# Second-stage matmuls of a fused attention and feed-forward kernel: 512 columns at once, or two times 256

## The chip, the core and the metric

The kernel runs on one core of one Trainium2 chip. The metric is the device time of one launch in microseconds (us). Five engines work side by side: TensorE (PE, matmuls; its weights loads are shown apart as PEld), VectorE (DVE), ScalarE (ACT), GpSimd (POOL) and SyncE (SP), which here only issues transfers. Data for the engines lie in on-chip memory; a matmul writes into accumulator banks, from which ScalarE and VectorE read the results.

## The reference

The reference computes a windowed attention over 8 batches, 8 heads, 576 positions and head size 64, in which a position sees itself and the 63 before it, and feeds the 4608 x 512 result through a feed-forward layer with a squared rectifier:

```python
scores = scale * np.matmul(q, k.transpose(0, 1, 3, 2))
mask = (rel >= 0) & (rel < window)              # window = 64
scores = np.where(mask, scores, -1000000000.0)
attn = np.exp(scores - np.max(scores, axis=-1, keepdims=True))
attn = attn / (np.sum(attn, axis=-1, keepdims=True) + 1e-09)
x = (attn @ v)  ->  4608 x 512
h = x @ w_in                                     # 512 x 2048
g = np.maximum(h, 0.0) ** 2
out = g @ w_out                                  # 2048 x 512
```

## The kernel before

The 4608 tokens are cut into 12 tiles of 384. A tile's feed-forward layer is 16 steps, one for each block of 128 hidden units. To keep accuracy with a fast one-pass number format (float32r), every factor is split into a high and a low part, and a product is the sum of three matmuls: high x high, high x low, low x high.

One step has two stages. In the **first stage** (`mm1`, line 352) twelve matmuls of 384 columns, four blocks of the 512 inputs with three products each, fill one bank, `h_ps`; the weights are blocks of `w_in`, and the tile's tokens stream past them. ScalarE takes the bank out with the rectifier (`r`, line 361), VectorE or ScalarE squares it (lines 366 and 364), ScalarE casts the high part (`ghi`, line 369) and VectorE subtracts to get the low part (`glo`, line 371). In the **second stage** (`mm2`, line 396) the blocks of 128 tokens of `ghi` and `glo` are the loaded weights, and the 512 columns of `w_out` stream past them: three token blocks with three products each, nine matmuls of 512 columns, each with a weights load of its own. They add up over the sixteen steps in three accumulators of 512 columns, one bank each: `oT` for the first token block and two buffers named `oV` for the others. After a tile's last step ScalarE copies each accumulator to `osb` (`put`, line 408), and SP sends it out (line 410). The streamed operand is read with its halves interleaved (`in_turn`), and the copies put the columns back in order (`by_half`, `ordered`).

TensorE also does the attention: scores (line 208), transposes of the probabilities (line 250) and products with the values (line 272). There are three such sections for each tile, and a section is worked into five steps of the feed-forward of an earlier tile.

Order: the first two tiles run in an order written out by hand (the string of tokens in the code), in which line 500 issues small filler matmuls on TensorE while data still arrive. From the third tile on, which is where the change acts, loops set the order. The second stage runs two steps behind the first: TensorE does `mm1` of step n, then the attention pieces of this step, then `mm2` of step n-2. Every engine works its instructions in the order in which they were issued; the weights load of a matmul is the one thing seen running beside the matmul ahead of it.

Of the kernel before, what the change touches and what calls it, by code (L numbers as in the profile page):

```python
# [24 lines left out]
def window_attention_relu2_ffn(ctx: ExitStack, tc: tile.TileContext, q, k, v, w_in, w_out, out):  # L25
    nc = tc.nc
    pe, dve, act, pool, sp = nc.tensor, nc.vector, nc.scalar, nc.gpsimd, nc.sync
    B, H, S, D = q.shape
    NT, DM = out.shape
# [3 lines left out]
    NF = DF // P  # L33
# [41 lines left out]
    wraw, wa, wparts = {}, {}, {}  # L75
# [299 lines left out]
    def in_turn(x):  # L375
        return x.rearrange("p (a b) -> p b a", a=2)

    def ordered(ps):
        return ps.rearrange("p (b a) -> p a b", a=2)

    def by_half(x):
        return x.rearrange("p (a b) -> p a b", a=2)

    hs, rg, gs, accs = {}, {}, {}, {}


    def mm2(t, f, ghi, glo):
        if f == 0 and t == 1:
            accs[t] = [ps_a.tile([P, 2, SW * P], F32, name=x)[:, n] for x, n in (("s_ps", slice(0, 2)), ("v_ps", 0))]
            accs[t] = [accs[t][0][:, 0], accs[t][0][:, 1], accs[t][1]]  # L390
        elif f == 0:
            accs[t] = [ps_o.tile([P, DM], F32, name="oV" if tb else "oT", bufs=2 if tb else 1) for tb in range(NTB)]
        for tb in range(NTB):
            ts = slice(tb * P, (tb + 1) * P)
            for n, (gg, part) in enumerate(((ghi, 0), (ghi, 1), (glo, 0))):
                pe.matmul(accs[t][tb], lhsT=gg[:, ts], rhs=in_turn(wparts[f][:, 1, part, :]),  # L396
                          start=f == 0 and n == 0, stop=f == NF - 1 and n == 2)
            if f == NF - 1 and t != 1:
                for op in "ZW":
                    put(op, t, tb)  # L400


    outs = {}

    def put(op, t, tb):
        if op == "Z":
            outs[t, tb] = wst.tile([P, DM], F32, name="osb", bufs=3)
            act.copy(by_half(outs[t, tb]), ordered(accs[t][tb]))
        else:
            sp.dma_start(out[t * TT + tb * P:t * TT + (tb + 1) * P, :], outs.pop((t, tb)))  # L410

# [93 lines left out]
    with tc.manual_schedule(engines={E.PE, E.DVE, E.Activation, E.Pool, E.SP}):  # L505
        for token in order.split():
            op, eng = token[0], token[-1] if token[-1] in "dap" else None
            n = int(token[1:].rstrip("dap"))
            if op in "LN":
                load_first("LN".index(op), n)  # L510
            elif op == "v":
                load_v(*divmod(n, (NB + 1) // 2))
            elif op == "w":
                fetch_w(n)
            elif op == "q":
                load_qk(1 + n // NPAIR, n % NPAIR)
            elif op == "D":
                turn(1 + n // NPAIR, n % NPAIR)
            elif op in "TU":
                ps_f[op, n] = turn_first("TU".index(op), *divmod(n, 2))  # L520
            elif op in "tu":
                copy_first("tu".index(op), *divmod(n, 2), ps_f[op.upper(), n], copier(eng))
            elif op == "K":
                idle(n)
            elif op in "abcdhl":
                weight(op, n)
            elif op == "M":
                hs[n] = mm1(*steps[n])
            elif op in "rpgG":
                evac(op, n, eng)  # L530
            elif op == "O":
                mm2(*steps[n], *gs.pop(n))
            elif op in "ZW":
                for tb in range(NTB):
                    put(op, steps[n][0], tb)
            else:
                section(op, n, eng)
# [4 lines left out]
    with tc.manual_schedule(engines={E.PE, E.DVE, E.Activation, E.Pool, E.SP}):  # L542
        for t in range(2, NTILE):
            for f in range(NF):
                n = NF * t + f
                m = min(f // 5, SPT - 1)
                hs[n] = mm1(t, f)
                evac("r", n)
                step(n, SPT * (t + 1) + m + 1, f - 5 * m)
                pend.append((n, t, f))  # L550
                done = pend.pop(0)
                mm2(*done[1:], *gs.pop(done[0]))
                if f != 5 * m:
                    for op in "pgG":
                        evac(op, n)
        for p in pend:
            mm2(*p[1:], *gs.pop(p[0]))
# [31 lines left out]
```

## Time and profile before

| what | value |
|---|---|
| median of 3 runs | 879.16 us (879.13 to 880.41) |
| span of the profiled execution | 878.4 us |
| TensorE matmuls: busy, count | 860.0 us, 6946 |
| TensorE weights loads: busy, count | 794.7 us, 6946 |
| VectorE, ScalarE, GpSimd busy | 452.0, 401.8, 50.1 us |
| mean granted TensorE clock | 0.996 |
| second-stage matmul of 512 columns, mean duration | 379 ns |
| first-stage matmul of 384 columns, mean duration | 327 ns |
| a 128x128 weights load, mean duration | 189 ns |

The profiled execution's own time is its span; the runs' median is 0.8 us above it. A matmul's duration in the profile reaches beyond the start of the next matmul, because they are pipelined; the distance from one start to the next is what adds up to time. In the groups, the columns are: line, engine, operation, output and inputs, shapes and count, then busy us and mean ns of one, then the idle time ahead of them and what ended it. In the timeline and the chain, the first number is the start in us from the beginning of the span and the second the length in us; several instructions in a row are merged, with their count.

### The profile page before, as it was taken

What the parts mean: (1) busy time and instruction counts of PE and PEld (TensorE: products, weight loads), DVE (VectorE), ACT (ScalarE), POOL (GpSimd) and SP (SyncE); (2) the same over time, 40 slices, a digit from 0 to 9 for tenths busy, and PEclk for the clock granted to TensorE, in tenths of its full rate; (3) what the DMA queues carried; (4) which work ended last, traced back from release to release, by engine and by line L of the source; (5) the groups of instructions that cost most, each with busy time, mean ns of one, the idle gap of its engine ahead of it and who ended that gap; (6) DMA issues with size and microseconds to landing.
All of it is one profiled execution on the core that took longest, in us unless ns stands there. A gap on an engine that the chain in (4) does not pass through costs nothing.

```text
span 878.4 us, 16976 instructions
## 1 busy us (share of the span) xinstructions
PE 860.0 (98%) x6946; PEld 794.7 (90%) x6946; DVE 452.0 (51%) x740; ACT 401.8 (46%) x1147; POOL 50.1 (6%) x70
## 2 busy tenths in 40 slices
PE   6799999999999999999999999999999999999998
PEld 5688998899999999999999999999999999999997
DVE  5799995754455444544455444453445544432222
ACT  5787875644344434434334444334434443432322
POOL 1210000210000000000000000000000000000000
PEclk9899999999999999999999999999999999999999
DMA  9989206460125002421033202141013200100100
GB/s 213 222 270 327 37 4 106 81 155 7 26 55 121 1 1 64 71 48 54 1 55 92 54 2 63 29 81 55 11 21 67 59 1 1 37 1 1 37 1 36
DMA packets 200302, 56.41 MB, mean 64 GB/s; under 512 B 185377, under 2 KB 193569, under 8 KB 200225
## 3 DMA queue, kind: packets, MB, share of 16 engines
q1 hardware_dynamic: 200224, 55.34, 27.4%
q8 instruction: 54, 0.88, 0.4%
q14 instruction: 24, 0.19, 0.1%
HBM read 45.88 MB, written 9.44 MB: 63 GB/s over the span
## 4 chain that ended last, share of the span: by engine, by line
PE 94%; SPq 3%; DMA 1%; ACT 1%; POOL 0%; DVE 0%; issue 0%; POOLq 0%
PE h_ps L352 42%; PE oV L396 26%; PE oT L396 14%; PE s_ps L208 3%; PE v_ps L272 3%; PE s_ps L396 2%; PE v_ps L250 1%; SPq L158 1%; PE v_ps L396 1%; SPq L130 1%; DMA w<-in_k_dram 1%; PE h_ps L500 0%; ACT sel L236 0%; SPq L80 0%; ACT r L361 0%
## 5 line engine op out<-in xcount | busy, mean ns | idle before, releaser
L352 PE MATMUL h_ps<-xhi,w 128*128 128x384 f32 x1536 | 407.0, 327 | 1.9 <-ACT r L361 1.4
L352 PEld LDWEIGHTS h_ps<-xhi,w 128*128 128x128 f32 x1536 | 275.2, 189 | 8.6 <-ACT r L361 3.3
L352 PE MATMUL h_ps<-xlo,w 128*128 128x384 f32 x768 | 250.6, 326 | 0.0
L361 ACT ACTIVATE r<-h_ps 128x384 f32<-128x384 f32 x192 | 93.6, 487 | 286.4 <-PE h_ps L352 285.7
L396 PE MATMUL oV<-w,ghi 128*128 128x512 f32 x704 | 209.5, 379 | 0.0
L366 DVE TENSOR_TENSOR r<-r 128x384 f32<-128x384 f32 x166 | 92.0, 554 | 165.4 <-ACT r L361 165.4
L371 DVE TENSOR_TENSOR glo<-r,ghi 128x384 fp32r<-128x384 f32 x192 | 107.8, 562 | 121.0 <-PE oV L396 82.0
L369 ACT CAST ghi<-r 128x384 fp32r<-128x384 f32 x192 | 98.8, 514 | 117.4 <-DVE r L366 115.4
L396 PEld LDWEIGHTS oV<-w,ghi 128*128 128x128 f32 x704 | 133.2, 189 | 18.8
L352 PEld LDWEIGHTS h_ps<-xlo,w 128*128 128x128 f32 x768 | 145.3, 189 | 4.8
L396 PE MATMUL oV<-w,glo 128*128 128x512 f32 x352 | 133.5, 379 | 0.0
L396 PE MATMUL oT<-w,ghi 128*128 128x512 f32 x352 | 110.2, 395 | 0.0
L236 ACT ACTIVATE sel<-sel,nm 128x64 f32<-128x64 f32 x272 | 90.8, 335 | 17.4 <-DVE nm L230 15.3
L396 PEld LDWEIGHTS oV<-w,glo 128*128 128x128 f32 x352 | 66.6, 189 | 9.4
L245 POOL TENSOR_TENSOR sel<-sel,rs 128x512 f32<-128x512 f32 x33 | 38.4, 1163 | 564.4 <-DVE rs L242 564.4
L396 PE MATMUL oT<-w,glo 128*128 128x512 f32 x176 | 66.8, 379 | 0.0
L254 DVE TENSOR_TENSOR pt<-v_ps,masks 128x1024 f32<-128x1024 f32 x31 | 38.0, 1224 | 46.8 <-PE v_ps L250 46.8
L396 PEld LDWEIGHTS oT<-w,ghi 128*128 128x128 f32 x352 | 59.0, 189 | 2.3 <-issue 0.2
L236 ACT ACTIVATION_READ_ACCUMULATOR sel<-sel,nm 128x1 f32 x272 | 50.9, 187 | 0.0
L140 DVE STREAM_TRANSPOSE qk<-raw 128x1152 f32<-128x1152 f32 x28 | 38.4, 1371 | 1.4 <-issue 1.4
L208 PE MATMUL s_ps<-qk 64*64 64x128 f32 (+1 forms) x1104 | 38.3, 276 | 0.1
L396 PEld LDWEIGHTS oT<-w,glo 128*128 128x128 f32 x176 | 33.3, 189 | 4.7
(80 smaller groups left out, 592.6 us busy)
## 6 DMA issues: line engine op xcount, KB each, us to landing
vt<-in_v_dram SPq DMA_DIRECT2D x144, 64.0 KB, 2.5
out_dram<-osb SPq DMA_DIRECT2D x36, 256.0 KB, 2.3
w<-in_moe_w_in_dram SPq DMA_DIRECT2D x16, 512.0 KB, 6.6
w<-in_moe_w_out_dram SPq DMA_DIRECT2D x16, 512.0 KB, 7.6
raw<-in_q_dram SPq DMA_DIRECT2D x112, 72.0 KB, 2.5
raw<-in_k_dram SPq DMA_DIRECT2D x112, 72.0 KB, 2.5
w<-in_q_dram SPq DMA_DIRECT2D x5, 256.0 KB, 4.6
w<-in_k_dram SPq DMA_DIRECT2D x5, 256.0 KB, 5.2
```

What stands on the lines that cost most here:

```text
L140: dve.transpose(get_turned(b, g // 2)[:, g % 2].rearrange("p n t -> p (n t)"), raw.rearrange("p n t -> p (n t)"))
L208: pe.matmul(ps[half * QB:(half + 1) * QB, j, w * P + c0:(w + 1) * P], lhsT=qk[r, 0, qb * QB:(qb + 1) * QB], rhs=qk[r, 1, k0:k0 + P - c0], ...
L236: act.activation(sels[i][:, w, hd], sels[i][:, w, hd], AF.Exp, bias=nms[i][:, n], scale=SCALE, accum_out=sums[i][:, n])
L245: (dve if eng == "d" else pool).tensor_tensor(p, p, rs[i][:, :, None].broadcast_to([P, SW * 2, QB]), ALU.mult)
L254: dve.tensor_tensor(pts[i].rearrange("p (w n) q -> p w n q", n=2), ps_t[i][:, :, None, :].broadcast_to([P, SW, 2, P]), masks.rearrange("p ...
L272: pe.matmul(ps[hd * D:(hd + 1) * D, j, q0:q0 + n * QB], lhsT=vts[b, kb // 2][r, kb % 2, 2 * d + hd, :], rhs=pts[i][r, n0:n0 + n, half * QB ...
L352: pe.matmul(h_ps, lhsT=wparts[f][:, 0, part, kk * P:(kk + 1) * P], rhs=in_turn(xx[:, kk, :]), start=n == 0, stop=n == 3 * NK - 1)
L361: act.activation(by_half(rg[n]), ordered(hs.pop(n)), AF.Relu)
L366: dve.tensor_tensor(rg[n], rg[n], rg[n], ALU.mult)
L369: act.copy(gs[n][0], rg[n])
L371: dve.tensor_tensor(gs[n][1], rg.pop(n), gs[n][0].bitcast(F32), ALU.subtract)
L396: pe.matmul(accs[t][tb], lhsT=gg[:, ts], rhs=in_turn(wparts[f][:, 1, part, :]), start=f == 0 and n == 0, stop=f == NF - 1 and n == 2)
```

## The change

From the third tile on (`t >= 2`), each second-stage matmul is issued as two: the first with the left 256 columns of the accumulator and of `w_out`'s block, the second with the right 256. Both have the same 128 token columns as weights, and each has a weights load. Within a half, the streamed operand is again read with its own two halves interleaved, so the evacuation is done by halves too: two copies of 256 columns in place of one of 512. The group is opened by the first half and closed by the second. The first two tiles, the first stage and the attention are as before.

```diff
         for tb in range(NTB):
             ts = slice(tb * P, (tb + 1) * P)
             for n, (gg, part) in enumerate(((ghi, 0), (ghi, 1), (glo, 0))):
-                pe.matmul(accs[t][tb], lhsT=gg[:, ts], rhs=in_turn(wparts[f][:, 1, part, :]),
-                          start=f == 0 and n == 0, stop=f == NF - 1 and n == 2)
+                if t < 2:
+                    pe.matmul(accs[t][tb], lhsT=gg[:, ts], rhs=in_turn(wparts[f][:, 1, part, :]),
+                              start=f == 0 and n == 0, stop=f == NF - 1 and n == 2)
+                else:
+                    for half in range(2):
+                        cs = slice(half * (DM // 2), (half + 1) * (DM // 2))
+                        pe.matmul(accs[t][tb][:, cs], lhsT=gg[:, ts], rhs=in_turn(wparts[f][:, 1, part, cs]),
+                                  start=f == 0 and n == 0 and half == 0, stop=f == NF - 1 and n == 2 and half == 1,
+                                  skip_group_check=True)
...
         if op == "Z":
             outs[t, tb] = wst.tile([P, DM], F32, name="osb", bufs=3)
-            act.copy(by_half(outs[t, tb]), ordered(accs[t][tb]))
+            for cs in (slice(0, DM),) if t < 2 else (slice(0, DM // 2), slice(DM // 2, DM)):
+                act.copy(by_half(outs[t, tb][:, cs]), ordered(accs[t][tb][:, cs]))
```

Line 396 of the kernel before is line 402 in the changed one for the tiles from the third on, and line 408 is line 416.

On TensorE, around the second stage of a step of the third tile, the kernel before has this order (line, operation, output and inputs, shape of the operand, count):

```order
L352 MATMUL h_ps<-xhi,w 128x384
L396 MATMUL oT<-w,ghi 128x512 x2
L396 MATMUL oT<-w,glo 128x512
L396 MATMUL oV<-w,ghi 128x512 x2
L396 MATMUL oV<-w,glo 128x512
L396 MATMUL oV<-w,ghi 128x512 x2
L396 MATMUL oV<-w,glo 128x512
L352 MATMUL h_ps<-xhi,w 128x384
```

The same place on TensorE in the changed kernel:

```order
L352 MATMUL h_ps<-xhi,w 128x384
L402 MATMUL oT<-w,ghi 128x256 x4
L402 MATMUL oT<-w,glo 128x256 x2
L402 MATMUL oV<-w,ghi 128x256 x4
L402 MATMUL oV<-w,glo 128x256 x2
L402 MATMUL oV<-w,ghi 128x256 x4
L402 MATMUL oV<-w,glo 128x256 x2
L352 MATMUL h_ps<-xhi,w 128x384
```

The group stands where it stood, between two first-stage groups, with eighteen matmuls in place of nine. In the whole program 1440 matmuls of 512 columns have become 2880 of 256.

On ScalarE, at the end of the third tile, the changed kernel has these rows with their waits (PE is TensorE; DMAHW are the transfers that free an `osb` buffer):

```order
L361 ACTIVATE r<-h_ps 128x384 [waits PE_49]
L416 COPY osb<-oT 128x256 [waits DMAHW1_49,PE_49]
L416 COPY osb<-oT 128x256
L416 COPY osb<-oV 128x256 [waits DMAHW2_49,PE_49]
L416 COPY osb<-oV 128x256
L416 COPY osb<-oV 128x256 [waits DMAHW3_49,PE_49]
L416 COPY osb<-oV 128x256
L369 CAST ghi<-r 128x384 [waits DVE_49]
```

Three copies have become six at the same place in ScalarE's queue; only the first of each pair has a wait.

## The prediction

> **What bounds the kernel now.** I read the page's totals first, then the chain of waits, then the timeline of one step of the loop.
>
> ```profile
> span 878.4 us, 16976 instructions
> PE 860.0 (98%) x6946; PEld 794.7 (90%) x6946; DVE 452.0 (51%) x740; ACT 401.8 (46%) x1147; POOL 50.1 (6%) x70
> PE 94%; SPq 3%; DMA 1%; ACT 1%; POOL 0%; DVE 0%; issue 0%; POOLq 0%
> ```
>
> TensorE is busy for nearly the whole span and is 94% of the chain that ends last; VectorE and ScalarE are about half used. So the time is the sum of TensorE's start-to-start distances (I call them pitches), and any change of a pitch goes straight into the end. The windows view says that this holds without gaps where the change acts, and at the full clock (columns: window, length, then busy time and count of PE, PEld, DVE, ACT, POOL, then the granted clock):
>
> ```profile
> 300.00:400.00 100.00, 100.00 (x791) 93.19 (x790) 46.99 (x86) 42.38 (x140) 4.81 (x4) 1.00 0.21 41
> 600.00:700.00 100.00, 100.00 (x855) 93.09 (x854) 47.43 (x87) 44.07 (x141) 4.60 (x4) 1.00 0.19 43
> ```
>
> The chain near the end, where no attention work is left, gives the pitches cleanly (start, length, what):
>
> ```profile
> 845.52 0.65 PE oT L396 x3
> 846.17 1.29 PE oV L396 x6
> 847.47 1.95 PE h_ps L352 x12
> ...
> 866.93 1.95 PE h_ps L352 x12
> 868.88 0.65 PE oT L396 x3
> ```
>
> From 845.52 to 868.88 lie six steps, so a step takes 23.36 / 6 = 3.893 us. Its twelve first-stage matmuls of 384 columns take 1.95 us, 162.5 ns each; that leaves 1.943 us for the nine second-stage matmuls of 512 columns, 215.9 ns each. The two forms lie on a line: (215.9 - 162.5) / 128 = 0.417 ns for a column, and 215.9 - 512 x 0.417 = 2.4 ns that every matmul pays whatever its width. The recorded durations are longer than the pitches, because neighbours overlap; only pitches add up.
>
> **The weights loads are hidden today.** The groups by form, and the timeline of one second-stage group:
>
> ```profile
> L352 PEld LDWEIGHTS h_ps<-xhi,w 128*128 128x128 f32 x1536 | 275.2, 189 | 8.6 <-ACT r L361 3.3 <-issue 0.3
> L396 PEld LDWEIGHTS oV<-w,ghi 128*128 128x128 f32 x704 | 133.2, 189 | 18.8
> L208 PEld LDWEIGHTS s_ps<-qk 64*64 64x64 f32 x1104 | 28.9, 136 | 8.0 <-issue 6.7 <-DVE qk L175 0.3 <-ACT ghi L369 0.3
> 503.57 0.59 PE L396 MATMUL oV<-w,ghi 128*128 128x512 f32 x2
> 503.79 0.19 PEld L396 LDWEIGHTS oV<-w,glo 128*128 128x128 f32 x1
> 504.00 0.38 PE L396 MATMUL oV<-w,glo 128*128 128x512 f32 x1
> ```
>
> The load for the matmul at 504.00 starts at 503.79, together with the matmul before it, and has that matmul's 215.9 ns to finish. A load of 128 columns shows 189 ns and one of 64 columns 136 ns, so 64 columns are worth 53 ns and 128 are worth about 106 ns; the rest is start-up. A load therefore has slack beside 512 columns (215.9) and beside 384 (162.5), and hardly any beside 256 columns, which by the line above last 256 x 0.417 + 2.4 = 109.1 ns. That is the disputed price: **the pitch of a stream of 256-column matmuls each with its own load.**
>
> No row of this kernel has that form, but three are near. The filler matmuls of line 500 are float32 passes of 128 columns with one 128x128 load each, at clock 1.00; the transposes of line 250 are 128 columns wide too, with a load of another kind (141 ns instead of 190):
>
> ```profile
> 9.70:10.85 1.15, 1.09 (x10) 1.15 (x10) 1.00 1.23 275
> 9.76 1.28 PE L500 MATMUL h_ps<-ident 128*128 128x128 f32 x10
> L500 PEld LDWEIGHTS h_ps<-ident x10: 190/192/193, 9.7 to 10.7; 128*128 128x128 f32 x10
> L500 PE MATMUL h_ps<-ident x10: 275/275/276, 9.8 to 10.8; 128*128 128x128 f32 x10
> L250 PE MATMUL v_ps<-ident,sel x4: 272/272/273, 520.5 to 520.8; 128*128 128x128 f32 x4
> 520.51 0.60 PE L250 MATMUL v_ps<-ident,sel 128*128 128x128 f32 x4
> L396 PEld LDWEIGHTS oT<-w,ghi x2: 190/191/192, 520.8 to 520.9; 128*128 128x128 f32 x2
> 520.84 0.30 PEld L396 LDWEIGHTS oT<-w,ghi 128*128 128x128 f32 x2
> ```
>
> Ten fillers take 1.28 us less the last one's own 0.275, over nine distances: 111.7 ns. Four transposes: (0.60 - 0.272) / 3 = 109 ns. Both stream 128 columns at what must be half the column rate (109 ns is the line's value for 256 columns), and they differ in the load: the lighter load leaves 109, the full one stretches it to 111.7. So a full 128x128 load is a resource that comes free every 111.7 ns. The last two rows show the same in this kernel's second stage: two of its loads stand 0.30 - 0.19 = 0.11 us apart, and the later one shows 192 ns, as in the fillers, where loads with room show 189. I take **111.7 ns**.
>
> **The change part by part.**
>
> *Matmuls.* Ten tiles of sixteen steps are changed, 160 steps. In each, nine matmuls become eighteen, every one with a 128x128 load, and the eighteen pitches run up to the first-stage matmul that follows, which also needs a full load. New: 18 x 111.7 = 2010.6 ns. Old: 1943 ns. The difference is 67.6 ns a step, **+10.8 us** in 160 steps. The columns streamed are the same; the sum is 18 extra fixed gaps less 9, plus 2.6 ns of load that no longer fits under each matmul. The bounds of the pitch: below, 109.1 ns (the load fits); above, 162.5 ns, since beside 384 columns the load does fit. Between these it is nearest to 111.7, because the load beside a full-rate stream (189 ns at lines 352 and 396) is no longer than beside the fillers (192).
>
> A page would have it lower. The Trainium skill, "TensorE: Matmul & The Clock Gate", section on LDWEIGHTS, counts a load as its columns divided by 1.2 per ns, 106.7 ns for 128; that is under 109.1, so by that rule the load stays hidden and the step costs what rival B says. The trace agrees with its slope (53 ns for 64 columns) but not with its sum: the fillers come at 111.7 ns.
>
> *What waits on TensorE.* Each step gets longer by 0.07 us, which only adds slack for the VectorE and ScalarE work of two steps later. These wait for TensorE, not the reverse:
>
> ```profile
> ACT r L361 <- PE h_ps L352: 285.7, 152, 3.9
> DVE glo L371 <- PE oV L396: 82.0, 91, 1.0
> PE h_ps L352 <- ACT r L361: 1.4, 3, 0.6
> ```
>
> *The evacuation.* Thirty ScalarE copies of 512 columns become sixty of 256. The second copy of a pair carries no wait of its own, so a pair starts when the whole accumulator is done, as before.
>
> ```profile
> L408 ACT COPY osb<-oV 128x512 f32<-128x512 f32 x22 | 12.9, 586 | 1.2
> L175 ACT COPY w<-oT 128x256 f32<-128x256 f32 x2 | 0.7, 372 | 0.5 <-PE oT L169 0.4
> 873.45 0.58 ACT L408 COPY osb<-oT 128x512 f32<-128x512 f32 x1 [2.90 <-PE oT L396]
> 874.10 1.23 ACT L408 COPY osb<-oV 128x512 f32<-128x512 f32 x2
> ```
>
> A pair costs 2 x 0.372 = 0.744 us against 0.586: 0.16 us more, 4.7 us over thirty, on an engine that is idle half the time. Inside the loop it is covered by the first-stage group (1.95 us) that stands between the last matmul of a tile and the first that reuses its bank; the casts queued behind it on ScalarE are wanted two steps later. Without that cover it would cost those 4.7 us. At the very end nothing covers it: three accumulators finish 0.65 to 0.67 us apart, and pairs of 0.744 us fall behind by 0.075 twice and then take 0.16 longer themselves. That is **+0.3 us**.
>
> *DMA and instructions.* The output transfers are unchanged in number and size. TensorE gets 1440 more loads and 1440 more matmuls, one instruction per 56 ns in the changed group. The attention sections already run denser, 72 loads and 72 matmuls in the 1.9 us from 506.91 on, so I put their issue at nothing:
>
> ```profile
> 506.91 0.86 PEld L208 LDWEIGHTS s_ps<-qk 64*64 64x64 f32 x32 [0.23 <-issue]
> 507.73 0.93 PEld L272 LDWEIGHTS v_ps<-pt,vt 64*64 64x64 f32 x40
> 508.73 0.70 PE L396 MATMUL oT<-w,ghi 128*128 128x512 f32 x2
> ```
>
> **Sum:** 10.8 + 0.3 = +11.1 us. The profiled span is 878.4 us and the median of the runs 879.16, so 0.8 us lie around the span; the forecast is 879.2 + 11.1 = **890.3 us**, 1.3% slower.
>
> **The rivals.**
>
> *A, the forecast:* the load sets the pitch. Readings of 111.2 to 112.2 ns give 889 to 892.
>
> *B, the load stays hidden:* the pitch is the line's 109.1. Then 18 x 109.1 = 1963.8 ns, 20.8 ns a step, 3.3 us, with the tail 3.6: **882.8 us**. For it: the transposes run at 109. Against it: their load is the lighter one. If the second load of a pair, which names the same weights again, were dropped on the way to the chip, the time would be this too.
>
> *C, no loss at all:* the 2.4 ns belong to a swap of weights and are not paid when the second half follows on the same weights. Its place is each pair of halves, which would then take 215.9 ns: only the tail is left, **879.5 us**. It decides once the mean pitch is under 108.4 ns (160 x (18 x 108.4 - 1943) = 1.3 us, and 0.3). For it: every matmul in the trace swaps weights, so the fixed part cannot be told from the swap. Against it: the halves each load anew. A gain beyond this would need columns cheaper than 0.417 ns, and 384 and 512 columns show the same price.
>
> *D, load and fixed gap add up,* because the stream now reads at full column rate beside the load where the fillers read at half: 111.7 + 2.4 = 114.1 ns, 110.8 ns a step, 17.7 + 0.3: **897.2 us**. Against it: the 189 ns beside full-rate streams.
>
> **How the numbers follow.** A 0.75, B 0.13, C 0.04, D 0.08 (with anything larger). The predicted time is A's. The range takes in B and A with some of the way to D: 882.5 to 894. A measurement of this kernel tells about 0.2%, 1.8 us, from no change; A, B and D all lie above that, C within: slower 0.95, same 0.04, faster 0.01.
>
> **What would show it.** In the new profile the matmuls of line 402 should start 111 to 112 ns apart, their loads show 192 ns instead of 189, a step outside attention take 3.96 us, and the clock stay at 1.00. Pitches of 109 with loads of 189 say B; a short step after a long one, C; 114, D. The last copy should end 0.9 us after the last matmul instead of 0.6. If TensorE shows idle time before the accumulators' first matmuls of a tile, the cover that I named for ScalarE is too thin, and if the clock falls, none of the sums hold.

## The result, and the profile after

The changed kernel takes 892.4 us (median of 4 runs, 891.94 to 893.0) against 879.78 us for the kernel before in the same set of runs: slower, ratio 1.0144 (95% interval 1.0131 to 1.0158). In a later set, with its own runs of the kernel before, it took 890.15 us against 879.4, ratio 1.0122 (1.0105 to 1.0139). The forecast was 890.3 us, a ratio of 1.0127.

The page of the changed kernel, its totals and its chain:

```profile
span 890.6 us, 19914 instructions
PE 871.0 (98%) x8386; PEld 844.5 (95%) x8386; DVE 452.0 (51%) x740; ACT 403.6 (45%) x1177; POOL 48.8 (5%) x70
PE 94%; SPq 3%; DMA 1%; ACT 0%; DVE 0%; issue 0%; ACTq 0%
```

TensorE is the bound as before, with 1440 more matmuls and 1440 more loads. The weights loads now fill 95% of the span where they filled 90%. The windows and the chain near the end show the new step:

```profile
300.00:400.00 100.00, 100.00 (x1045) 98.45 (x1044) 45.40 (x82) 40.25 (x127) 4.81 (x4) 1.00 0.21 41
845.12 0.67 PE oT L402 x6
845.78 1.34 PE oV L402 x12
847.12 1.95 PE h_ps L352 x12
...
868.88 0.67 PE oT L402 x6
```

TensorE still has no gap and the clock is 1.00. Six steps now take 868.88 - 845.12 = 23.76 us, 3.960 us each, where they took 3.893. The first stage keeps its 1.95 us. The eighteen second-stage matmuls take 0.67 + 1.34 = 2.01 us, 111.7 ns each. By lines, the loads and matmuls of the second stage read:

```profile
L402 PEld LDWEIGHTS oV<-w,glo x640: 192/192/192, 196.4 to 886.4; 128*128 128x128 f32 x160
L402 PE MATMUL oV<-w,glo x640: 275/275/275, 196.5 to 886.5; 128*128 128x256 f32 x160
L352 PEld LDWEIGHTS h_ps<-xhi,w 128*128 128x128 f32 x1536 | 276.4, 190 | 4.1 <-ACT r L361 2.9
```

The loads of the second stage show 192 ns, the mark that the filler matmuls had before, and the 256-column matmuls show the fillers' 275 ns. The first-stage loads average 190 ns where they averaged 189: those right behind a second-stage group show 192 too.

**Where the 12.6 us lie.** A marker that both kernels reach with the same code is the first evacuation of the second tile, the copies out of `s_ps`. From its start to the start of the last second-stage matmul, before and after (the times are the first and last starts of a group):

```profile
L408 ACT COPY osb<-s_ps x2: 579/584/588, 142.1 to 142.6; 128x512 f32<-128x512 f32 x2
L396 PE MATMUL oV<-w,glo x352: 378/379/380, 50.5 to 874.3; 128*128 128x512 f32 x176
```

```profile
L416 ACT COPY osb<-s_ps x2: 578/583/588, 143.4 to 143.8; 128x512 f32<-128x512 f32 x2
```

Before: 874.3 - 142.1 = 732.2 us. After: 886.5 - 143.4 = 743.1 us. The difference, 10.9 us, is what the change costs. The other 1.3 us of the 12.2 us between the two spans had arisen before the marker, in code that the change leaves alone; the remaining 0.4 us of the 12.6 is the difference between spans of single executions and medians. The profiles of the experiments reach this marker between 139.4 and 142.8 us, so it moves by itself from execution to execution.

### The profile page after: what moved, and what is told of

Read it like the earlier page. It is cut to its first block, busy times and chain, and to the rows that moved or that the text cites. A ratio compares the mean times of both kernels' runs of the same rounds, so it can differ in the third digit from the quotient of the medians.

```text
span 890.6 us, 19914 instructions
## 1 busy us (share of the span) xinstructions
PE 871.0 (98%) x8386; PEld 844.5 (95%) x8386; DVE 452.0 (51%) x740; ACT 403.6 (45%) x1177; POOL 48.8 (5%) x70
## 4 chain that ended last, share of the span: by engine, by line
PE 94%; SPq 3%; DMA 1%; ACT 0%; DVE 0%; issue 0%; ACTq 0%
PE h_ps L352 42%; PE oV L402 24%; PE oT L402 13%; PE v_ps L272 3%; PE s_ps L208 3%; PE s_ps L397 2%; PE oV L397 2%; SPq L130 1%; PE v_ps L250 1%; PE oT L397 1%; SPq L158 1%; PE v_ps L397 1%; DMA w<-in_k_dram 1%; DMA w<-in_moe_w_in_dram 1%; SPq L80 0%; SPq L79 0%
## 5 line engine op out<-in xcount | busy, mean ns | idle before, releaser
L402 PE MATMUL oV<-w,ghi 128*128 128x256 f32 x1280 | 195.2, 275 | 0.0
L402 PEld LDWEIGHTS oV<-w,ghi 128*128 128x128 f32 x1280 | 168.6, 192 | 0.0
L402 PE MATMUL oV<-w,glo 128*128 128x256 f32 x640 | 123.7, 275 | 0.0
L402 PE MATMUL oT<-w,ghi 128*128 128x256 f32 x640 | 102.1, 282 | 0.0
L402 PEld LDWEIGHTS oV<-w,glo 128*128 128x128 f32 x640 | 97.1, 192 | 0.0
L402 PEld LDWEIGHTS oT<-w,ghi 128*128 128x128 f32 x640 | 89.2, 191 | 1.8
L402 PE MATMUL oT<-w,glo 128*128 128x256 f32 x320 | 61.9, 275 | 0.0
L402 PEld LDWEIGHTS oT<-w,glo 128*128 128x128 f32 x320 | 48.6, 192 | 0.0
```

The lines of the kernel that those rows point to most:

```text
L402: pe.matmul(accs[t][tb][:, cs], lhsT=gg[:, ts], rhs=in_turn(wparts[f][:, 1, part, cs]), start=f == 0 and n == 0 and half == 0, stop=f == N ...
```

## The experiments

Theory L is the prediction's: a full 128x128 load needs 111.7 ns, only one load can run ahead of its matmul, and so a matmul narrower than some 262 columns, (111.7 - 2.4) / 0.417, waits for the next load. The rivals put the cost elsewhere: in a larger fixed gap of a narrow matmul (G), in loads that queue up and have to fit only in the mean (Q), in a difference between loading new weights and loading again what is there already (W), in the evacuation (E), or in the changed program as such (S).

**Uneven pieces: 384 and 128 columns**

```diff
-                    for half in range(2):
-                        cs = slice(half * (DM // 2), (half + 1) * (DM // 2))
-                        pe.matmul(accs[t][tb][:, cs], lhsT=gg[:, ts], rhs=in_turn(wparts[f][:, 1, part, cs]),
...
+                    for c0, c1 in CUTS:
+                        pe.matmul(accs[t][tb][:, c0:c1], lhsT=gg[:, ts], rhs=in_turn(wparts[f][:, 1, part, c0:c1]),
...
-            for cs in (slice(0, DM),) if t < 2 else (slice(0, DM // 2), slice(DM // 2, DM)):
+            for cs in (slice(0, DM),) if t < 2 else [slice(*c) for c in CUTS]:
...
+    CUTS = ((0, 384), (384, 512))
```

In a diff, `...` stands for lines that are not shown. The diffs are against the changed kernel unless said otherwise. The evacuation is cut at the same columns as the matmuls.

> Each second-stage matmul from the third tile on is split into 384 and 128 columns in place of 256 and 256; same number of matmuls, loads and columns. Theory L (a full 128x128 load needs 111.7 ns and only the next load can run beside a matmul): the 384 piece keeps its 162.5 ns, the 128 piece is stretched from 55.7 to 111.7 ns, 274.2 ns a pair, (274.2 - 215.9) x 9 x 160 = +84 us on the kernel before, about 964 us. Rival G (a narrow matmul pays a larger fixed gap, 4.9 ns in place of 2.4, and the load has nothing to do with it): as 256 and 256, about 892 us. Rival Q (loads queue up further ahead and only their mean has to fit): 2 x 111.7 = 223.4 ns a pair, about 892 us.

Measured: 964.39 us (one run). The chain of this kernel:

```profile
927.45 2.01 PE h_ps L352 x12
929.46 0.77 PE oT L401 x6
930.23 1.65 PE oV L401 x12
931.87 0.22 PE h_ps L352
```

From 927.45 to 931.87 a step takes 4.42 us, 0.53 more than before, as theory L has it (9 x 58.3 ns = 0.525). The first stage shows 2.01 us here instead of 1.95, because its first matmul waits for its load; the last section shows such a wait. As many matmuls and loads as in the change, and as many columns, cost 85 us in place of 11. So the cost does not hang on the number of matmuls (against G), and the slack that a load leaves beside 384 columns cannot be used by the load after it (against Q): one load is ahead, not two.

**Four pieces of 128 columns**

Against the kernel with 384 and 128 columns:

```diff
-    CUTS = ((0, 384), (384, 512))
+    CUTS = ((0, 128), (128, 256), (256, 384), (384, 512))
```

> Each second-stage matmul from the third tile on is four of 128 columns, each with its own load. Theory L: 4 x 111.7 = 446.8 ns in place of 215.9, (446.8 - 215.9) x 9 x 160 = +332 us, about 1212 us, with starts 111.7 ns apart. Rival G (4.9 ns of fixed gap for each matmul): 213.5 + 4 x 4.9 = 233 ns, +25 us, about 905 us.

Measured: 1212.29 us (one run). The loads by line, and the chain:

```profile
L401 PEld LDWEIGHTS oV<-w,ghi x2560: 192/192/192, 194.9 to 1205.9; 128*128 128x128 f32 x197
1180.72 2.01 PE h_ps L352 x12
1182.72 1.28 PE oT L401 x12
1184.01 2.68 PE oV L401 x24
1186.69 2.01 PE h_ps L352 x12
```

A step takes 1186.69 - 1180.72 = 5.97 us. Less the first stage's own 1.95 (the 2.01 shown again holds a wait for a load) that is 4.02 us for 36 matmuls, 111.7 ns each: a matmul of 128 columns has the same pitch as one of 256. With half the streaming beside each load, the load is no faster, so the stream does not slow the load down; this speaks against the prediction's rival D as well.

**A shorter load under the same 256 columns**

```diff
                 else:
+                    rows = P if f == 0 else 96
                     for half in range(2):
                         cs = slice(half * (DM // 2), (half + 1) * (DM // 2))
-                        pe.matmul(accs[t][tb][:, cs], lhsT=gg[:, ts], rhs=in_turn(wparts[f][:, 1, part, cs]),
+                        pe.matmul(accs[t][tb][:rows, cs], lhsT=gg[:, tb * P:tb * P + rows], rhs=in_turn(wparts[f][:, 1, part, cs]),
```

> As the change, but from the second step of a tile on the weights are 96 of the 128 token columns, so 32 of each 128 tokens get only the first step's sum; left out is that work. The streamed columns and the number of matmuls stay. Theory L: the load is 32 columns shorter, 32 x 0.83 = 27 ns, so it shows about 165 ns and fits; the starts stand 109.1 ns apart in 150 of 160 steps, 150 x 18 x 2.6 = 7.0 us less than the change, about 885.4 us, ratio to the kernel before about 1.006. Rival G: 111.7 ns as before, about 892 us, ratio 1.014.

Measured: 883.3 us (median of 6), ratio to the kernel before 1.0049 (1.0031 to 1.0067).

```profile
L403 PEld LDWEIGHTS oV<-w,ghi x1280: 162/163/192, 194.4 to 877.6; 128*96 128x96 f32 x171, 128*128 128x128 f32 x12
L403 PE MATMUL oV<-w,ghi x1280: 272/273/275, 194.6 to 877.7; 128*96 128x256 f32 x171, 128*128 128x256 f32 x12
842.91 1.95 PE h_ps L352 x12
844.86 0.66 PE oT L403 x6
845.52 1.31 PE oV L403 x12
...
862.50 1.95 PE h_ps L352 x12
```

From the second step of a tile on, this kernel leaves out the last 32 tokens of each 128. It is the run that separates the load from the matmul: streamed columns and counts are the change's, and the load is shorter. It shows 162 to 163 ns in place of 192, the matmul falls from 275 to 272 or 273, and five steps take 862.50 - 842.91 = 19.59 us, 3.918 each: (3.918 - 1.95) / 18 = 109.3 ns. Against the later set's 890.15 us the kernel is 6.9 us faster, where 7.0 were expected; the expected 885.4 us was counted down from the first set's 892. Of the 4.0 us that remain over the kernel before, the fixed gaps of the added matmuls explain 3.1 (150 steps of 20.8 ns), and the ten steps with full loads 0.7.

The same trace holds both loads side by side, because the first step of each tile keeps the full one. The first matmuls of two steps of one tile, and the first-stage matmuls behind these steps:

```profile
544.12 0.61 PE L403 MATMUL oT<-w,ghi 128*128 128x256 f32 x4
546.12 0.33 PE L352 MATMUL h_ps<-xhi,w 128*128 128x384 f32 x1
552.43 0.60 PE L403 MATMUL oT<-w,ghi 128*96 128x256 f32 x4
554.40 0.33 PE L352 MATMUL h_ps<-xhi,w 128*128 128x384 f32 x1
```

Eighteen matmuls take 546.12 - 544.12 = 2.00 us with the full load and 554.40 - 552.43 = 1.97 us with the short one, 111 against 109 ns each. With 96 columns of weights a matmul also has 96 rows of output instead of 128. That its columns become no cheaper by this is seen from its pitch, which falls on the line drawn through matmuls with 128 rows (109.1 ns).

**All three products of one half first**

```diff
-                else:
-                    for half in range(2):
-                        cs = slice(half * (DM // 2), (half + 1) * (DM // 2))
...
+            for half in range(2 if t > 1 else 0):
+                cs = slice(half * (DM // 2), (half + 1) * (DM // 2))
+                for n, (gg, part) in enumerate(((ghi, 0), (ghi, 1), (glo, 0))):
...
```

> As the change, but all three products of the left half come before those of the right half, so that no two matmuls in a row have the same weights. Theory L: a load costs the same whatever it loads, starts 111.7 ns apart, about 892 us. Rival W (a load of the weights that are there already differs from a load of new ones): another pitch, for example 114 ns where the weights change and 109 where they don't in the change, and here 114 throughout, +6 us, about 898 us.

Measured: 890.67 us (one run), and the chain shows the change's own step:

```profile
869.07 1.95 PE h_ps L352 x12
871.03 0.67 PE oT L402 x6
871.69 1.34 PE oV L402 x12
873.03 0.98 PE h_ps L352 x6
```

From 869.07 to 873.03 lie 3.96 us. The new order does less than was expected of it: the first two products of a half both load `ghi`, so two matmuls in a row still have the same weights there. Of the six matmuls of a token block, four follow on their own weights in the change and two do here. Under rival W, with its 114 and 109 ns, this shift alone would have made the step 0.03 us longer, and it did not. The change's own trace shows the pitch on unchanged weights directly:

```profile
865.42 0.61 PE L402 MATMUL oV<-w,ghi 128*128 128x256 f32 x4
865.87 0.39 PE L402 MATMUL oV<-w,glo 128*128 128x256 f32 x2
866.09 0.61 PE L402 MATMUL oV<-w,ghi 128*128 128x256 f32 x4
```

The four `ghi` matmuls load the same 128 token columns: (0.61 - 0.275) / 3 = 111.7 ns from start to start. The six pitches from 865.42 to 866.09, two of which lead to new weights, take 0.67 us, 111.7 ns each as well. Loading the same weights again costs what loading others costs; rival W falls.

**The evacuation alone**

Against the kernel before:

```diff
-            act.copy(by_half(outs[t, tb]), ordered(accs[t][tb]))
+            if t < 2:
+                act.copy(by_half(outs[t, tb]), ordered(accs[t][tb]))
+            else:
+                for b in range(2):
+                    bs = slice(b * DM // 4, (b + 1) * DM // 4)
+                    act.copy(by_half(outs[t, tb])[:, :, bs], ordered(accs[t][tb])[:, :, bs])
```

> The kernel before with its second-stage matmuls left whole; only ScalarE's evacuation is done in two copies of 256 columns from the third tile on. Theory: the copies are off TensorE's path, and only the last pair is in the open: at most +0.3 us, ratio 1.000. Rival E (the copies hold up the next tile's first accumulation or the casts behind them): some of the 4.7 us that thirty longer pairs cost, ratio up to 1.005, and TensorE idle before line 396's first matmul of a tile.

Measured: 879.44 us against 879.4, ratio 0.9993 (0.998 to 1.0006): no difference that the runs can tell. The copies of this kernel at its end:

```profile
873.72 0.65 ACT L413 COPY osb<-oT 128x256 f32<-128x256 f32 x2 [2.91 <-PE oT L396]
874.37 1.29 ACT L413 COPY osb<-oV 128x256 f32<-128x256 f32 x4
```

A pair takes 0.65 us, not the 0.744 of two copies end to end: the second starts while the first still finishes.

**Half the dose**

```diff
-                if t < 2:
+                if t < 7:
...
-            for cs in (slice(0, DM),) if t < 2 else (slice(0, DM // 2), slice(DM // 2, DM)):
+            for cs in (slice(0, DM),) if t < 7 else (slice(0, DM // 2), slice(DM // 2, DM)):
```

> The change from the eighth tile on only, 80 steps in place of 160. Theory: 80 x 67.5 ns = +5.4 us on the kernel before in the span between the first changed step and the end, ratio 1.006; of the 1.8 us by which the change was slower than its steps explain, the part that belongs to start-up and not to the change stays within the spread of the runs. Rival S (the changed program as such costs something outside its steps): +5.4 and up to 1.8 more, ratio 1.008.

Measured: 885.82 us, ratio 1.0069 (1.0049 to 1.009), within both expectations, so the time alone does not decide. The profile does:

```profile
L416 ACT COPY osb<-s_ps x2: 579/584/589, 139.4 to 139.9; 128x512 f32<-128x512 f32 x2
L402 PE MATMUL oV<-w,glo x320: 275/275/275, 541.0 to 877.2; 128*128 128x256 f32 x160
```

From the marker to the last matmul: 877.2 - 139.4 = 737.8 us, 5.6 more than the kernel before (732.2) by these rounded starts, of which the steps explain 5.4. That leaves next to nothing for rival S behind the marker, and before it the changed kernels come no later as a rule (139.4 to 143.4 us, the kernel before 142.1). This execution reached the marker 2.7 us earlier than the kernel before in its profile, in unchanged code.

**The change once more**

> The change once more, beside the two above. Theory: 160 x 67.5 ns = +10.8 us in the steps, the last copy about 0.1 us later, and the rest of the difference to the kernel before is in the first 60 us, where it moves from run to run with the half-clock stretches: ratio 1.012 to 1.015.

Measured: 890.15 us, ratio 1.0122 (1.0105 to 1.0139). Its profile:

```profile
L416 ACT COPY osb<-s_ps x2: 578/583/588, 142.8 to 143.3; 128x512 f32<-128x512 f32 x2
L402 PE MATMUL oV<-w,glo x640: 275/275/275, 195.9 to 885.9; 128*128 128x256 f32 x160
```

885.9 - 142.8 = 743.1 us, the same as in the first profile to 0.1 us. The two profiled executions are 0.8 us apart (892.61 and 891.82 us), and 0.6 us of that lie before the marker. The medians of the two sets differ by 2.25 us; where the rest of that lies is not shown.

## Why the prediction was right

*The bound.* TensorE's pitches add up to the time: right. The step's growth appears undiminished at the end, and the work that waits for TensorE only gained slack.

*The pitch of 111.7 ns.* Right, and for the stated reason. It was taken from ten filler matmuls near the start of the trace, with another number format, half the columns and a mean over nine distances; the change gave the same 111.7 ns over the eighteen matmuls of a step. That a distance seen with float32 would hold for float32r was argued from the 192 ns of two loads, not known. The decisive step was to ask which resource two near rows differ in: the transposes and the fillers have the same width and differ in the load. Shortening the load brought the pitch down to 109.3 ns, so the cause is shown, not only the number.

*The matmul term.* +10.8 us forecast, 10.9 measured from marker to last matmul.

*The evacuation.* That it is covered inside the loop was right (ratio 0.9993 with the copies alone). Its tail was mis-sized: +0.3 us forecast, from two copies end to end. The last rows of the chain of the changed kernel, and its last copies in the timeline:

```profile
886.82 0.37 ACT osb L416
886.15 1.32 ACT L416 COPY osb<-oV 128x256 f32<-128x256 f32 x4
```

The last matmul started at 886.5 and shows 0.275 us, so it ends at 886.8, and the last copy ends at 886.15 + 1.32 = 887.47, 0.7 us later, where the prediction had 0.9 and the kernel before 0.6. The last pair started at 886.82 and took 0.65 us rather than 0.744, less than the 0.67 us in which the next accumulator becomes ready, so nothing piled up. Of the +0.3 us, about 0.1 came.

*The rivals.* B (load hidden) needed 109.1 ns, and only the load of 96 columns came near it (109.3). C (no cost for a second half on the same weights) and D (114.1 ns) do not appear in any kernel. C could have been struck out beforehand. The prediction says that every matmul in the trace swaps weights, and that is a misreading: the two `ghi` products of a token block follow on the same weights in the kernel before too. By the starts in its trace they stand 215.8 ns apart (some 420 places without attention work ahead), as do the matmuls that follow on new weights; C needed 213.5. The Trainium skill's figure for a load, columns divided by 1.2 per ns ("TensorE: Matmul & The Clock Gate", section on LDWEIGHTS), is right in slope here (27 to 29 ns less for 32 columns fewer: 162 or 163 ns against 189 or 192) but is short by 5 ns as the distance of one load from the next, 111.7 against 106.7, and these 5 ns decide between B and A.

*What was not foreseen.* The first set of runs came out 2 us above the forecast and the second at it. Of the first profile's 12.2 us, 1.3 lie in the start-up, which no term of the sum held. That the second median (890.15) meets the forecast to 0.2 us is in part luck: the tail was over-sized by 0.2 us, and the runs of that set lie between 889.12 and 891.82. The prediction took 0.2% for what a measurement can tell from no change; the ratio's two intervals are 0.27% and 0.34% wide, and two medians of the same kernel lay 0.25% apart. The 0.8 us that the prediction puts around the span compares the profiled execution with the median of others; where both are on record for one execution (892.61 and 890.6, 880.13 and 878.4), it is 1.7 to 2.0 us. The forecast does not rest on it, since it adds to the median.

No version faster than the kernel before came out of the runs: the widest matmul hides its load with room, and each further cut adds either a fixed gap or a load in the open.

## What to carry to other kernels

Compare the pitch of a matmul (start to start, from the chain, not the recorded duration) with the distance at which loads can follow one another, taken from a place in the same trace where loads stand close together. While the matmul lasts longer (here at 384 and 512 columns), its load is free; once it is shorter (here at 256 and 128) the load sets the pitch whatever the width, and slack beside a wide neighbour does not help, since only one load is ahead. A cut that leaves every piece just at that limit costs little (1.2 to 1.4% here); one that leaves a piece far below it costs much (9.7% with 384 and 128 columns).

## What the runs showed of the hardware

The pitch of narrow matmuls with full loads is flat: 111.7 ns at 256 columns and at 128. A matmul that waits for its weights does not show idle time ahead of it. Its record starts on time and is longer. In the kernel with 384 and 128 columns the two widths show this together:

```profile
900.73 0.22 PE L401 MATMUL oV<-w,glo 128*128 128x128 f32 x1
900.79 0.38 PE L352 MATMUL h_ps<-xhi,w 128*128 128x384 f32 x1
901.00 0.33 PE L352 MATMUL h_ps<-xlo,w 128*128 128x384 f32 x1
```

The 384-column matmul behind the 128-column one starts 0.06 us after it, shows 0.38 us instead of 0.33, and the next one starts 0.21 us later instead of 0.16: the 0.05 us of waiting for the load stand inside the record. TensorE's busy share therefore says nothing of it: it is 98% of the span before, after and with 384 and 128 columns, and 99% with four pieces. Only the pitches tell.
